# A fused transformer block on one Trainium2 core: six weight loads of the first MLP chunk move from ahead of the out-projection's copies to behind them

## The chip, the core and the metric

The kernel runs on one NeuronCore of one Trainium2 chip. The core has a matrix engine (PE), a vector engine (DVE), an activation engine (ACT), a general engine (POOL) and a sync engine (SP), which in this kernel issues nearly all DMAs, in program order. A DMA that SP has issued runs on the core's 16 DMA engines, and an instruction that needs its data waits on a semaphore. The metric is device time in microseconds (us), lower is better, and a difference is told from no change from about 0.2% on.

## The reference, cut to what matters

```python
x = A_x                                        # 2048 tokens x 640
sa, ca, ga, sb, cb, gb = split(silu(c) @ w_mod)
h = layernorm(x) * (1 + ca) + sa
q, k, v = split(h @ wqkv)                      # 32 heads of 20
o = softmax(q @ k.T / sqrt(20)) @ v            # per head, 2048 x 2048 scores
x = x + ga * (o @ wo)                          # out-projection
h = layernorm(x) * (1 + cb) + sb
out = x + gb * (((h @ w_gate) * (h @ w_up)) @ w_down)   # MLP, 640 -> 1536 -> 640
```

## The kernel before

**Chunks, items, groups.** The 2048 query rows are cut into five chunks of 512, 512, 512, 256 and 256 rows. A chunk has eight items, one for each set of four heads. An item's scores come in units of 128 keys by up to 512 queries; PE writes them into PSUM (L1443), and their exponential is taken either on ACT, two units (later sometimes three) at a time into the tile PP (L1479: one such instruction is an "exp group"), or on DVE, by an integer approximation that goes through the tiles DB and DSS (L1503, L1535, L1540, L1543). PE then multiplies PP or DSS with the values Vf (L2000).

**What follows a chunk.** When an item is done, DVE turns its result out of PSUM (L1627), POOL scales it (L1633), DVE turns it again into OcT (L1641), and four or five DMAs copy OcT's rows to their places in Ocp (L1654). Once a chunk's eight items are in Ocp, `suffix(ci)` follows: eight rounds of the out-projection (PE, L906 with wo and Ocp; the result is added to xck at L1725), a layer norm (L1739 to L1746), five rounds of transposes into h2T (L1758), then for each of 12 column blocks fc a gate round and an up round (L906 with h2T and stg), and the down-projection. All this PE work is laid between the score groups of the next chunk, so the out-projection and MLP of chunk 0 run while chunk 1's exps run.

**The weight blocks.** Gate and up weights come in blocks of 128 columns (160 KB each, L1798) into `stg`, which has three places for gate and three for up blocks. So the first six blocks (fc 0, 1, 2, gate and up) can be requested at once, and each later block must wait until a round has released its place.

**What sets the order.** The program is laid out by a planner at build time. `Sched` simulates the engines with assumed costs, and whenever an engine is free in the simulation it takes the ready task with the lowest priority number whose gate is open. What comes out is a fixed instruction order for each engine, with semaphore waits for every dependence; the simulated times themselves are not in the program. A gate is a number of exp groups: a task may be taken once that many groups have begun in the simulation. Chunk 0 has 512 units, less 4 for each of its 24 quads on DVE, so 416 on ACT, in 208 groups: `gstart[1]`, and with it `gb` of chunk 0, is 208. The gates of chunk 0 that matter here:

| tasks | line | gate | priority on SP |
|---|---|---|---|
| x rows for the residual (xck) | L1704 | gb - 20 = 188 | 15 |
| first six gate and up blocks | L1798 | gb - 10 = 198 | 16.00 to 16.02 |
| copies OcT to Ocp | L1654 | none (ready when OcT is) | 2 |
| first out-projection round | L1732 | gb + 9 = 217 | not on SP |
| first gate round | L1853 | 229, from the same formula at L1697 | not on SP |

On SP lie also, at this place, the projected queries of the last quarter of the tokens: they go from the tile KPB to a DRAM scratch q_rows (L1212, priority 1.5) and come back from it as QT (L1234, priority 1.6) once the rows have landed.

Of the kernel before, what the change touches and what calls it, by code (L numbers as in the profile page):

```python
# [8 lines left out]
BF16 = mybir.dt.bfloat16  # L9
# [7 lines left out]
PV_W = 216.0  # L17
# [100 lines left out]
class Sched:  # L118

    def __init__(self):  # L120
        self.tasks = []
        self.order = {k: [] for k in ("sp", "act", "pe", "dve", "pool")}
        self.all = []
        self.free_at = {k: T0 for k in self.order}
        self.pend = {k: [] for k in self.order}
        self.readyl = {k: [] for k in self.order}
        self.t = 0.0
        self.n = 0
        self.progress = 0
        self.dma_free = 0.0  # L130
        self.pe_mode = None
        self.pe_end = 0.0
        self.pick_pe = None
        self.every = []
        self.ham_w = 0
        self.ham_act = 0.0
        self.cold = True
        self.ncold = 0
        self.nfill = 0
        self.ndup = 0  # L140
        self.nsteal = 0
        self.nx = 0
        self.ng = 1 << 30
        self.hist = []
        self.acts = []
        self.left = 0
        self.lk_end = {"dve": 0.0, "pool": 0.0}
        self.lk_last = None
# [337 lines left out]
GATE_F = (0.468, 0.693, 0.969, 0.732, 1.0)  # L486
FILL_MIN = 4153.722
FILL_HARD = 0.0
FILL_T0, FILL_TH, FILL_MINH = 2300.0, 17000.0, 7500.0
FILL_MODE = 'P'  # L490
DUP_MIN = 0.0
# [54 lines left out]
    39: {"FILL_MIN": 3000, "D_LATE": 17, "PVTOL": 258, "X_LATE": -54.236, "PVCAP": 16},  # L546
}
XHALF = 1
X_LATE = -24.052
X_HALF = 0.0  # L550

# [9 lines left out]
def build_kernel(nc, A_x, A_wqkv, A_wo, B_x, B_w_gate, B_w_up, B_w_down, c, w_mod, out):  # L561
# [7 lines left out]
    NC = len(CHUNKS)  # L569
# [6 lines left out]
    sc = Sched()  # L576
# [14 lines left out]
    def alloc(name, shape, dtype):  # L591
        off = cur[0]
        cur[0] += nb(shape, dtype)
        assert cur[0] <= nc.sbuf_top, f"SBUF overflow at {name}: {cur[0]} > {nc.sbuf_top}"
        return at(name, shape, dtype, off)
# [17 lines left out]
    ps = nc.alloc_psum_tensor("ps_all", [128, 8, 512], F32)  # L613
# [7 lines left out]
    ident = alloc("ident", [128, 128], BF16)  # L621
    mhalf = alloc("mhalf", [128, 4], F32)
    warm = alloc("warm", [128, 1], F32)
    qcol = alloc("qcol", [128, 1], F32)
    c5 = alloc("c5", [KD, 128], BF16)
    csb = alloc("csb", [128, KD], BF16)
# [109 lines left out]
    BPV = 7  # L736
# [15 lines left out]
    def dve(dur, f, deps=(), prio=3.0, **k):  # L752
        return sc.add(Task("dve", dur, f, deps, prio=prio, **k))
# [6 lines left out]
    def pool(dur, f, deps=(), prio=3.0, **k):  # L760
        t = Task("pool", dur, f, deps, prio=prio, **k)
        t.lk = 1
        return sc.add(t)
# [63 lines left out]
    def load_rest():  # L827
# [5 lines left out]
        for q, f in enumerate((first2[0], first2[1],  # L833
# [13 lines left out]
    p_id = pool(300, lambda e: e.affine_select(ident[:], ident[:], pattern=[[-1, 128]], compare_op=ALU.not_equal,  # L847
                                               fill=1.0, base=0, channel_multiplier=1), [p_i0], prio=0)
    p_mh = pool(100, lambda e: e.memset(mhalf[:], -0.5), prio=1)
    p_on = dve(600, lambda e: e.memset(Vf[:, :].rearrange("p (h w) -> p h w", w=VW)[:, :, 0:1], 1.0), prio=-1)  # L850
    d_pz = dve(500, lambda e: e.memset(ps[:, BPV, :], 0.0), [], prio=3.5)
    d_wz = [dve(70, lambda e, w=w: e.memset(w[:, :, D:WKQ], 0.0), prio=0) for w in (wk_sb, wq_sb)]
# [233 lines left out]
    v_last = []  # L1086
# [179 lines left out]
    items = [(ci, j) for ci in range(NC) for j in range(NSET)]  # L1266
# [3 lines left out]
    item_info = {}  # L1270
# [51 lines left out]
    gstart = []  # L1322
# [129 lines left out]
    st_pv = {"item": 0, "free": [d_pz]}  # L1452
# [57 lines left out]
    for qi, (it, us) in enumerate(dquads):  # L1510
# [36 lines left out]
        if X_POOL and qi % X_POOL == X_POOL - 1 and qi < len(dquads) - X_LAST and all(  # L1547
                dquads[z][0] == it for z in range(qi, min(len(dquads), qi + X_TAIL + 1))):
            st_["xby"] = None
            for x in range(X_PIECES):  # L1550
# [5 lines left out]
                t = Task("pool", w * POOL_NS + 180.0, fxp, [tm, te], prio=2.0 + .1 * qi + .01 * x, name=f"XP.{qi}")  # L1556
# [13 lines left out]
            t = term(fx, [tm, te], TT_2X, "X", src=0, last=True)  # L1570
# [106 lines left out]
    def suffix(ci):  # L1677
        alt = NALT and ci >= NC - 2
        bd = bset_done[1 if NALT and ci == NC - 2 else 0]
        hprod, h2T, xck, xn2 = set_r if not alt else set_t if ci == NC - 2 else set_c  # L1680
        first = bd.get("tr", [])
        if alt:
            first = list(sfx_done["qd1"]) if ci == NC - 2 else bd["tr"] + bd["h2T"] + bd["hp"] + bd["out"]
# [3 lines left out]
        tail = ci == NC - 1  # L1687
        qf = full if tail and TAILX else quarters
        t0 = q0 // 128
        gb = int(gstart[ci + 1]) if not tail else 0  # L1690
# [11 lines left out]
        def pr(early=False):  # L1702
            return pbase + rc_[0] - (1500 if tail and early else OPFIRST if early else 0)
        d_xc = dma("sp", 128 * ntl * D * 2, lambda e: e.dma_start(xck[:, 0:ntl, :], xv[:, t0:t0 + ntl, :]),  # L1704
                   (first if alt else bd.get("out", []) + v_last), prio=15, gate=max(0, gb - 20))
        t_xn2 = []
        x1_done = []
        op_last = []
        for tl in range(ntl):
            ev = []  # L1710
            for hf in range(2):
# [12 lines left out]
                def after(r, tl=tl, hf=hf, fx=fx, pq=pq):  # L1724
                    f = lambda e: e.tensor_tensor(xck[:, tl, 320 * hf:320 * hf + 320], ps[:, r.b["b"], 0:320],  # L1725
                                                  xck[:, tl, 320 * hf:320 * hf + 320], ALU.add)
                    if tail and OP_EARLY:
# [5 lines left out]
                          name=f"op{ci}.{tl}")  # L1733
                ev.append(r.evac[0])
                op_last.append(r.last)
            t = t0 + tl
# [52 lines left out]
        for fc in range(FT):  # L1789
            use_x = tail and fc < nsx  # L1790
            wbuf, dm = [], []
            for w_, wv in enumerate((wgv, wuv)):
                cell = {}
                if use_x:
                    cell["t"] = stx[fc][:, w_, :, :]

                def f(e, wv=wv, fc=fc, cell=cell):
                    return e.dma_start(cell["t"], wv[:, :, fc * 128:(fc + 1) * 128])  # L1798
                t = dma("sp", 2 * 128 * KD * 128 * 2, f, sfx_done["qdead"] if use_x and fc < nsq else first if use_x else kp_use if ci == 0 else [], prio=16 + ci + .01 * fc,
                        gate=int(gstart[NC] - 40) if tail and not use_x else 0 if tail else max(0, gb - 10))  # L1800
                if not use_x:
                    t.acq = [(sStg[w_], "s", 1)]

                    def on0(task, cell=cell, w_=w_):
                        cell["i"] = task.slots["s"]
                        cell["t"] = stg[cell["i"]][:, w_, :, :]
                    t.on_start = on0
                wbuf.append(cell)
                dm.append(t)
# [29 lines left out]
            for w_ in range(2):  # L1839
# [5 lines left out]
                if w_ == 0:  # L1845
                    def after(r, gs=gs):
# [3 lines left out]
                        if tail:  # L1850
# [3 lines left out]
                              name=f"g{ci}.{fc}")  # L1854
# [13 lines left out]
        for tl in range(ntl):  # L1868
# [4 lines left out]
            for (c_, w) in cuts:  # L1873
# [10 lines left out]
                if tail and TAILX:  # L1884
# [6 lines left out]
                            prio=1))  # L1891
# [7 lines left out]
    for it in range(len(items)):  # L1899
        ci, j = items[it]  # L1900
# [5 lines left out]
    pvstate = {"sidx": 0, "didx": 0}  # L1906
# [12 lines left out]
    def clk():  # L1919
        return 2.0 if sc.cold else 1.0  # L1920

    def mode_start(mode, t):
        if sc.pe_mode is not None and sc.pe_mode != mode:
            return max(t, sc.pe_end + (PE_BACK if sc.pe_mode == 'S' else PE_SWITCH))
        return max(t, sc.pe_end)

    def s_ready():
        g = pvstate["sidx"]
        if g >= NG:
            return None  # L1930
        ts, us = score_q[g]
        r = 0.0
        for d in ts.deps:
            if d.done is None:
                return None
            r = max(r, d.done + SEM)
        for pool, key, refs in ts.acq:
            a = pool.avail()
            if a is None:
                return None  # L1940
            r = max(r, a[0])
        return r
# [265 lines left out]
    def pick_pe(t):  # L2208
# [4 lines left out]
        if g < NG:  # L2213
# [4 lines left out]
            if (g != HEADG or not HEADG or back[0]) and acquire_ready(ts, t):  # L2218
                start = mode_start("S", t)
# [19 lines left out]
        if dst["next"] < len(dlist) and (g >= NG or due[dst["next"]] + D_LATE < apos[g]):  # L2239
# [3 lines left out]
            if d_attach(ts, t, 1e9, rows, 2, False):  # L2243
                start = mode_start("S", t)
# [17 lines left out]
        sr = s_ready()  # L2262
        if HOLD and sr is not None and t < sr <= t + HOLD and ring() >= RINGLOW:
            return half_x(t)
        if sc.recent(t) < FILL_MIN and ring() >= RINGLOW and pick_x(t, True):
            return True
        if sc.recent(t) < FILL_HARD and t > 20000 and do_fill(t):
            return True
# [6 lines left out]
        it = st_pv["item"]  # L2275
# [32 lines left out]
        if cands and not js and len(cands) >= 2 and (not PV0 or it >= PV0N or len(cands) >= PV0 or cands[0][0] == 'd'):  # L2308
            pv_issue(cands, t)
            return True  # L2310
        if t > FILL_T0 and fill_ok(t, fill_deps):
            return do_fill(t)
        return False

    def do_fill(t):
        mode = FILL_MODE if pvstate["sidx"] else "X"
        start = mode_start(mode, t)
        fs = G
        if pvstate["sidx"] == 0:
            fs = next((q for q in (GX, GC) if q.avail() is not None and q.avail()[0] <= t), GC)  # L2320
        task = Task("pe", 216.0, ffill, fill_deps, ctr="pex", mode=mode, name="fill", acq=[(fs, "g", 1)])
        if not sc.acquire(task, t):
            return False
        b_ = task.slots["g"]
        idb = ident[:].unsqueeze(1).to_broadcast([128, 4, 128])
        if mode == "X":
            task.emits = [lambda e: e.matmul(ps[:, b_, :].rearrange("p (a b) -> p a b", a=4), ident[:], idb)]  # L2327
        else:
            task.emits = [lambda e, x=x: e.matmul(  # L2329
                ps[32 * x:32 * x + 32, b_, :].rearrange("p (a b) -> p a b", a=4), ident[:, 32 * x:32 * x + 32], idb,  # L2330
                tile_position=(0, 32 * x), skip_group_check=True) for x in range(4)]
        sc.activity(start, 512.0)
        sc.left += 1
        sc.finish_issue(task, start, 216.0 * clk())
        fs.done(b_, task)
        sc.pe_mode = mode
        sc.pe_end = start + 216.0 * clk()
        sc.free_at["pe"] = sc.pe_end
        sc.nfill += 1
        return True  # L2340

    fill_deps = [p_id]
    ffill = None

    def fill_ok(t, fdeps):
        if any(d.done is None or d.done + SEM > t for d in fdeps):
            return False
        if xcur[0] is not None and not (PASSDEP or HT0_SPLIT):
            return False
        return sc.recent(t) < (FILL_MINH if t < FILL_TH else FILL_MIN)  # L2350
# [54 lines left out]
```

## Time and profile before

| | us |
|---|---|
| median of 3 runs | 816.97 (816.37 to 817.6) |
| span of the profiled execution, first to last instruction | 821.3 |
| ACT busy in the span | 775.3 (94%), of it 756.2 in 775 exps (L1479) |
| PE busy in the span | 793.6 (97%) |
| DVE busy in the span | 720.4 (88%) |
| six weight blocks issued on SP | 219.87 to 223.15 |
| first out-projection matmul of chunk 0 | 232.33 |
| first gate matmul of chunk 0 | 268.3 |

The profile is of one execution, and it doesn't give that execution's own device time; what lies around its span can only add to it, so it took at least 821.3, and that is 4.3 above the median of the runs. Its times count from the span's start. "Idle before" an instruction is the time its engine had nothing to do ahead of it, and the name behind the arrow is what it waited for. PEclk is the clock that the throttle granted to PE, as a share of full speed. SPq rows are the instructions that issue DMAs; their length is the issue alone, not the transfer.

### The profile page before, as it was taken

The page shows a single profiled execution, that of the slowest core. Times are in us where ns is not written, and L with a number is a line of the kernel's source. Part 1 is how long each engine was busy: PE and PEld are TensorE (multiplying, and loading weights), DVE is VectorE, ACT ScalarE, POOL GpSimd, SP SyncE. Part 2 cuts the span into 40 slices and gives each one's busy share as a digit, 9 for nine tenths or more (in the row PEclk, how much of TensorE's full clock was granted, in tenths as well). Part 3 has the DMA queues.
Part 4 walks back from the last instruction along what each step waited for, and adds up shares of the span by engine and source line. Part 5 has one row for each costly group of instructions (what it writes and reads, how often), then busy time and mean ns, then how long its engine had stood idle before and what let it go on. Part 6 is the DMA issues. An engine that isn't in the chain of part 4 may idle for free.

```text
span 821.3 us, 28879 instructions
## 1 busy us (share of the span) xinstructions
PE 793.6 (97%) x12493; PEld 305.9 (37%) x12493; DVE 720.4 (88%) x1275; ACT 775.3 (94%) x818; POOL 79.1 (10%) x105
## 2 busy tenths in 40 slices
PE   9999999999989999999999999999988999999998
PEld 4433333322223223233233232333143444554567
DVE  7989999899989999999999999998798877667753
ACT  6899999999989999999999999999899999999941
POOL 3300000020002000000011000000011000001000
PEclk9999999999999999999999999999699999999999
DMA  9734211114500235000300222000400236105610
GB/s 292 219 85 104 67 45 40 50 33 123 131 18 25 54 99 138 22 11 23 92 7 6 53 54 54 6 21 23 82 8 10 50 87 134 47 30 127 137 42 17
DMA packets 116445, 54.71 MB, mean 67 GB/s; under 512 B 83915, under 2 KB 116319, under 8 KB 116319
## 3 DMA queue, kind: packets, MB, share of 16 engines
q1 hardware_dynamic: 115391, 51.72, 24.9%
q8 instruction: 99, 1.62, 0.8%
q10 hardware_dynamic: 928, 1.15, 0.4%
q14 instruction: 27, 0.22, 0.1%
HBM read 41.85 MB, written 8.41 MB: 61 GB/s over the span
## 4 chain that ended last, share of the span: by engine, by line
PE 43%; ACT 35%; DVE 15%; issue 7%; DMA 0%; SPq 0%; POOL 0%; DVEq 0%; ACTq 0%; POOLq 0%
ACT PP L1479 34%; PE ps_all L1443 13%; PE ps_all L906 13%; PE ps_all L2000 9%; DVE DB L1503 5%; PE ps_all L902 3%; DVE DSS L1540 3%; DVE DSS L1543 2%; DVE DSS L1535 1%; PE ps_all L2327 1%; PE ps_all L1166 1%; PE ps_all L1102 1%; PE ps_all L1063 1%; DVE wd L1429 1%; DVE gsb L1847 1%
## 5 line engine op out<-in xcount | busy, mean ns | idle before, releaser
L1479 ACT ACTIVATE PP<-ps_all 128x1024 bf16<-128x1024 f32 (+1 forms) x775 | 756.2, 1171 | 11.6 <-PE ps_all L1443 10.0
L1443 PE MATMUL ps_all<-QT,KT 32*128 32x512 bf16 (+1 forms) x2560 | 311.4, 343 | 16.6 <-ACT PP L1479 10.9
L1503 DVE TENSOR_SCALAR DB<-ps_all 128x512 int16<-128x512 f32 x400 | 265.0, 682 | 43.7 <-PE ps_all L1443 42.9
L1443 PEld LDWEIGHTS ps_all<-QT,KT 32*128 32x128 bf16 x2560 | 81.3, 91 | 264.9 <-ACT PP L1479 228.4
L2000 PE MATMUL ps_all<-PP,Vf 128*32 128x512 bf16 (+2 forms) x2084 | 166.0, 346 | 0.4 <-DVE OT L1627 0.4
L1540 DVE TENSOR_TENSOR DSS<-DB,DSS 128x2048 bf16<-128x2048 bf16 x100 | 122.6, 1226 | 0.0
L906 PE MATMUL ps_all<-h2T,stg 128*32 128x512 bf16 (+1 forms) x1740 | 116.8, 347 | 0.9 <-DVE DB L1503 0.2
L1633 POOL TENSOR_TENSOR OTn<-OT,invT 128x512 bf16<-128x512 f32 (+1 forms) x39 | 46.6, 1195 | 604.5 <-DVE invT L1631 604.5
L2000 PE MATMUL ps_all<-DSS,Vf 128*32 128x512 bf16 (+3 forms) x952 | 78.5, 354 | 1.0 <-DVE DSS L1540 0.5
L2000 PEld LDWEIGHTS ps_all<-PP,Vf 128*32 128x32 bf16 (+1 forms) x2084 | 46.0, 94 | 89.8 <-issue 82.0
L1535 DVE TENSOR_SCALAR DSS<-DB 128x2048 int16<-128x2048 int16 x100 | 70.6, 706 | 0.8
L1543 DVE TENSOR_SCALAR DSS<-DB 128x2048 int16<-128x2048 int16 x100 | 69.0, 690 | 0.3 <-PE ps_all L2000 0.3
L906 PE MATMUL ps_all<-wd,hprod 128*32 128x320 bf16 (+1 forms) x1316 | 58.5, 284 | 0.1
L906 PEld LDWEIGHTS ps_all<-h2T,stg 128*32 128x32 bf16 x1740 | 39.2, 96 | 35.0 <-issue 18.2
L906 PEld LDWEIGHTS ps_all<-wd,hprod 128*32 128x32 bf16 x1316 | 31.2, 96 | 16.6 <-issue 7.4
L2000 PEld LDWEIGHTS ps_all<-DSS,Vf 128*32 128x32 bf16 (+1 forms) x952 | 24.0, 95 | 25.1 <-issue 14.3
L906 PE MATMUL ps_all<-wV,hT 128*32 128x320 bf16 (+1 forms) x704 | 32.3, 289 | 0.1
L1166 PE MATMUL ps_all<-hT,wq 128*32 128x512 bf16 x375 | 31.6, 382 | 0.1
L906 PE MATMUL ps_all<-wo,Ocp 128*32 128x320 bf16 (+1 forms) x628 | 28.6, 290 | 1.9 <-DMA Ocp<-OcT 1.8
L2329 PE MATMUL ps_all<-ident 128*32 128x512 bf16 x300 | 28.6, 406 | 0.3 <-DVE DB L1503 0.2
L1847 DVE CAST gsb<-ps_all 128x512 bf16<-128x512 f32 x36 | 24.5, 681 | 3.0 <-PE ps_all L906 3.0
L1627 DVE STREAM_TRANSPOSE OT<-ps_all 128x512 f32<-128x512 f32 (+1 forms) x40 | 24.1, 603 | 2.8 <-PE ps_all L2000 2.7
(122 smaller groups left out, 509.1 us busy)
## 6 DMA issues: line engine op xcount, KB each, us to landing
stg<-in_B_w_gate_dram SPq DMA_DIRECT2D x50, 160.0 KB
stg<-in_B_w_up_dram SPq DMA_DIRECT2D x50, 160.0 KB
QT<-q_rows SPq DMA_DIRECT2D x22, 128.0 KB
KT<-k_rows SPq DMA_DIRECT2D x84, 32.0 KB
wm<-in_w_mod_dram SPq DMA_DIRECT2D x3, 800.0 KB
x<-in_A_x_dram SPq DMA_DIRECT2D x7, 320.0 KB
xck<-in_A_x_dram SPq DMA_DIRECT2D x3, 640.0 KB
wd<-in_B_w_down_dram SPq DMA_DIRECT2D x1, 1920.0 KB
```

What stands on the lines that cost most here:

```text
L906: return lambda e, b: e.matmul(ps[32 * x:32 * x + 32, b, c0 + o:c0 + o + w], lhs()[:, 32 * x:32 * x + 32], rhs() if w == n else rhs()[:, o ...
L1166: f = [lambda e, b_, k=k, x=x: e.matmul(ps[x:x + min(32, w - x), b_, :], wx[:, k, r0 + x:r0 + min(x + 32, w)], hT[tc][:, k, :], tile_posit ...
L1443: ems.append(lambda e, i=i, kt=kt: e.matmul(dstf()[:, i * u.n:(i + 1) * u.n], KT[32 * u.s:32 * u.s + 32, u.j, kt * 128:(kt + 1) * 128], QT ...
L1479: return e.activation(PPs[g % 2][:, cellp["p"], 0:nu * 512], ps[:, b0:b0 + nu, :].rearrange("p b c -> p (b c)"), AFT.Exp, scale=ESCALE)
L1503: return e.tensor_scalar(DB0[:, st_["slot"], x * 512:(x + 1) * 512], bank(cell["b"]), EBIAS, 0.0, op0=ALU.add, op1=ALU.max)
L1535: return e.tensor_scalar(DSS[:, st_["ss"][0], :], DB0[:, st_["slot"], :], 0x7F, 0x3F00, op0=ALU.bitwise_and, op1=ALU.bitwise_or)
L1540: return e.tensor_tensor(d, DB0[:, st_["slot"], :].bitcast(BF16), d, ALU.mult)
L1543: return e.tensor_scalar(DSS[:, st_["ss"][1], :], DB0[:, st_["slot"], :], 0x7F80, 2, op0=ALU.bitwise_and, op1=ALU.bitwise_or)
L1633: f3 = lambda e: e.tensor_tensor(OTn[:, 0:n].rearrange("p (b c r) -> p b r c", c=32, r=2), OT[:, 0:n].rearrange("p (b r c) -> p b r c", c= ...
L1847: f = lambda e: e.tensor_copy(gsb[:, gs, 0:n], ps[:, r.b["b"], 0:n])
L2000: ems.append(lambda e, i=i, kt=kt, stt=stt, stp=stp: e.matmul(ps[32 * s:32 * s + mc, BPV, 0:u.n], Vf[:, (kt * H + 4 * u.j + s) * VW:(kt * ...
L2329: task.emits = [lambda e, x=x: e.matmul(ps[32 * x:32 * x + 32, b_, :].rearrange("p (a b) -> p a b", a=4), ident[:, 32 * x:32 * x + 32], id ...
```

## The change

The gate of the gate and up loads becomes a parameter for chunk 0 (`STG_G0`) and one for the others (`STG_G`). For chunk 0 it goes from gb - 10 to gb + 12, that is from group 198 to group 220. For the other chunks it stays at gb - 10, and the gate of the xck load, now a parameter too, stays at gb - 20.

```diff
+STG_G0, STG_G, XC_G = 12, -10, -20
...
-                   (first if alt else bd.get("out", []) + v_last), prio=15, gate=max(0, gb - 20))
+                   (first if alt else bd.get("out", []) + v_last), prio=15, gate=max(0, gb + XC_G))
...
-                        gate=int(gstart[NC] - 40) if tail and not use_x else 0 if tail else max(0, gb - 10))
+                        gate=int(gstart[NC] - 40) if tail and not use_x else 0 if tail else max(0, gb + (STG_G0 if ci == 0 else STG_G)))
```

The diff also brings a second kind of filler matmul (`zero_fill`), which is off: its threshold `FILL_Z` is 0, so neither its matmuls nor the memset of its tile are emitted.

```diff
+FILL_Z, Z_LATE = 0.0, 0.0
...
+    zt = alloc("zt", [128, 32], BF16)
...
+    p_zt = pool(100, lambda e: e.memset(zt[:], 0.0), prio=5) if FILL_Z > 0.0 else None
...
-        if t > FILL_T0 and fill_ok(t, fill_deps):
-            return do_fill(t)
-        return False
+        if t > FILL_T0 and fill_ok(t, fill_deps) and do_fill(t):
+            return True
+        return FILL_Z > 0.0 and sc.recent(t) < FILL_Z and zero_fill(t)
```

The tile `zt` (64 bytes in each partition) is allocated all the same, so every tile allocated behind it lies 64 bytes further on.

More of the change, by code (lines that the diff above doesn't have):

```diff
@@ L141, in __init__ @@
         self.nsteal = 0
+        self.nzero = 0
         self.nx = 0
@@ L2310, in pick_pe, with zero_fill @@
             return True
-        if t > FILL_T0 and fill_ok(t, fill_deps):
-            return do_fill(t)
-        return False
+        if t > FILL_T0 and fill_ok(t, fill_deps) and do_fill(t):
+            return True
+        return FILL_Z > 0.0 and sc.recent(t) < FILL_Z and zero_fill(t)
+    def zero_fill(t):
+        it = st_pv["item"]
+        if it >= len(items) or pvstate["sidx"] < 2 or not item_info[it]["started"] or t < FILL_TH or p_zt.done is None:
+            return False
+        start = mode_start("P", t)
+        sr = s_ready()
+        if sr is not None and start + PV_W > sr + Z_LATE:
+            return False
+        idb = ident[:].unsqueeze(1).to_broadcast([128, 4, 128])
+        task = Task("pe", 216.0, [lambda e, x=x: e.matmul(
+            ps[32 * x:32 * x + 32, BPV, :].rearrange("p (a b) -> p a b", a=4), zt[:], idb,
+            tile_position=(0, 32 * x), start=False, stop=False, skip_group_check=True) for x in range(4)],
+            [p_zt, p_id], ctr="pep", mode="P", name="zfill")
+        task.seq = 0
+        sc.activity(start, 512.0)
+        sc.left += 1
+        sc.finish_issue(task, start, PV_W * clk())
+        sc.pe_mode = "P"
+        sc.pe_end = start + PV_W * clk()
+        sc.free_at["pe"] = sc.pe_end
+        sc.nzero += 1
+        return True
     def do_fill(t):
```

## The prediction

> **What bounds the kernel now.** I read the page first: the chain that ended last is ACT's exps for 34% of the span and PE for 43%, and ACT is 94% busy. I then asked for the busy time of each engine in stretches of 10 us. From 240 to 570 ACT has almost no gap (0.11 at 320, 0.28 at 480, 0.22 at 540), so there a microsecond that ACT loses is a microsecond of the end. ACT loses much in three places only: 2.67 in 230 to 240, 0.98 + 2.19 in 570 to 590, and 1.29 in 630 to 640. The change lies at the first. The timeline of the SP queue around it (start, length, line, DMA):
>
> ```profile
> 219.87 0.44 SPq L1798 DMA_DIRECT2D stg<-in_B_w_gate_dram  x1
> ...
> 222.62 0.53 SPq L1798 DMA_DIRECT2D stg<-in_B_w_up_dram  x1
> 223.24 1.26 SPq L1212 DMA_DIRECT2D q_rows<-KPB  x2
> 227.16 0.83 SPq L1234 DMA_DIRECT2D QT<-q_rows  x2
> 228.03 3.05 SPq L1654 DMA_DIRECT2D Ocp<-OcT  x4
> 244.47 1.61 SPq L1212 DMA_DIRECT2D q_rows<-KPB  x3
> 247.85 2.85 SPq L1234 DMA_DIRECT2D QT<-q_rows  x4
> ```
>
> The timeline of all engines:
>
> ```profile
> 220.82 0.68 DVE L1178 TENSOR_SCALAR KPB<-ps_all 128x512 bf16<-128x512 f32 x1
> ...
> 223.59 0.43 DVE L1641 STREAM_TRANSPOSE OcT<-OTn 128x256 f32<-128x256 f32 x1
> ...
> 230.18 0.39 PE L1443 MATMUL ps_all<-QT,KT 32*128 32x512 bf16 x2
> ...
> 232.33 0.73 PE L906 MATMUL ps_all<-wo,Ocp 128*32 128x320 bf16 x16 [1.76 <-DMA Ocp<-OcT]
> ...
> 233.65 1.02 ACT L1479 ACTIVATE PP<-ps_all 128x1024 bf16<-128x1024 f32 x1 [1.69 <-PE ps_all L1443]
> ...
> 235.26 1.02 ACT L1479 ACTIVATE PP<-ps_all 128x1024 bf16<-128x1024 f32 x1 [0.59 <-PE ps_all L1443]
> ...
> 236.68 4.70 ACT L1479 ACTIVATE PP<-ps_all 128x1024 bf16<-128x1024 f32 x5 [0.39 <-PE ps_all L1443]
> ```
>
> PE is through at 230.57 and stands until 232.33, because its next instruction is the first out-projection round and the copies to Ocp have not landed. The scores of the next exp are behind that round, so ACT runs dry for 1.69, and then twice more, 0.59 and 0.39: together 2.67. The last two come from the clock. By stretches (PE, PEld, DVE, ACT, POOL busy, then granted clock, DMA share, GB/s):
>
> ```profile
> 230.00:232.00 2.00, 0.57 (x6) 0.10 (x2) 1.53 (x2) 1.96 (x3) 0.00 (x0) 1.00 0.13 31
> 232.00:234.00 2.00, 1.67 (x27) 0.65 (x31) 0.35 (x1) 0.35 (x1) 0.00 (x0) 0.75 0.03 8
> 234.00:236.00 2.00, 2.00 (x26) 0.49 (x18) 1.83 (x4) 1.41 (x2) 0.00 (x0) 0.50 0.02 4
> 236.00:238.00 2.00, 2.00 (x44) 0.78 (x36) 1.09 (x2) 1.61 (x3) 0.00 (x0) 0.90 0.00 0
> ```
>
> PE gets half its clock right after the gap, for about 3.4 us.
>
> **Why the copies are late.** OcT is done at 224.02, yet its copies are issued from 228.03, since SP works in order. KPB is ready at 221.50, but its stores are issued only at 223.24, because SP issues weight blocks until 223.15. The stores end at 224.50, and SP can go on only at 227.16, when they have landed: 2.66 later. The two other places with these stores show 1.77 (246.08 to 247.85) and 1.74 (266.53 to 268.27). What differs is the traffic: the DMA share is 1.25 and 1.08 in 222 to 226, with the weight blocks, and 0.20 (246 to 248) and 0.11 (264 to 268) at the other two.
>
> **The change, part by part.**
>
> *Where the six loads go.* The new gate, 220, opens when the exp of group 219 begins. The profile counts 217 exps up to 224.0 and 222 up to 228.0, so that is at about 226. The copies to Ocp are ready at 224.02, before it, and have priority 2 against 16, so the planner places the loads behind all four. The next SP task is the store at 244.47; six loads at 0.55 each (3.28 before) fill 3.3 us of a hole of 13, so nothing behind them on SP is displaced. Only SP's order changes, then: out of the run behind QT, to behind the fourth copy. The number of DMAs is the same.
>
> *The chain without them.* SP is free at 219.82, after the QT loads. The stores go at 221.54 (KPB plus 0.04, as at 244.43 to 244.47) and end at 222.80. They land 1.75 later, at 224.55 (by the undisturbed rows; by the disturbed one, 2.66, at 225.46). QT: 224.55 to 225.38. Ocp: 225.42 to 228.48 (3.05 long as now). The first round was released 1.20 after the last copy's issue ended (231.09 to 232.29), so now at **229.68**, or 230.59 by the other end. PE gets there at 230.57. The wait of 1.76 is gone, with 0.9 to spare by the one end and 0.02 short by the other.
>
> *The loads' new place.* They go at 228.5 to 231.9. The same six blocks of chunk 1, issued at 391.44, keep the DMA engines busy until about 398, so they take some 7 us: landed by 235.5. The first gate round needs them at 268.3, now 265.6: 30 us of cover. Against the last Ocp copy they come behind it in the queue; if they slowed its landing as they now slow the stores, by 0.9, it would be 230.6, again no wait worth naming. Later blocks wait for a place that a round frees, which doesn't change. By the Trainium skill, "DMA: Bandwidth & Descriptors", section "Rules for kernel authors", a DMA is to be issued early and waited for late. That speaks against this change; here it would price the lost head start, and the rows price it at nothing, since 30 us remain.
>
> *What is late next.* The copies no longer bind; ACT's own exps do. Around chunk 1's first out-projection (419.5, no wait for Ocp) ACT is busy 10.00 of 10 in every stretch, with the same rounds between the same kind of groups. So I take the whole 2.67 as won, and none lost to the next limit.
>
> *The rest.* The filler is off, and no instruction comes of it. Tiles lie 64 bytes further on. No row shows a price for an address; I take 0, from the argument that no shape changes, with 0.1 either way as bound.
>
> **Sum.** ACT saves 1.69 + 0.59 + 0.39 = 2.67. The profiled execution would have a span of 818.6 in place of 821.3; put against the median of the runs, 816.97 - 2.67 = **814.3**. The step from one to the other is not free: the runs are at least 4.3 faster than the profiled execution, so some of its stalls aren't in them. Taking out the two stalls at 570 to 590 and 630 to 640 (3.17 + 1.29 = 4.46) would explain that, and so nearly would the one here with the last (2.67 + 1.29 = 3.96). I take the first, because the stall here follows from the order on a queue and the two others follow no long wait of PE.
>
> **The rivals.**
>
> *Only the wait is won (815.3).* The half clock could be no consequence of the wait, or be absent in the runs. At 574 to 588 and 629 to 632 the clock is halved with no such wait before, so it does come on its own. Then ACT wins 1.69: 816.97 - 1.69 = 815.28. For it also stands a rule: the Trainium skill, "TensorE: Matmul & The Clock Gate", section "Why this matters for your kernels", holds gaps under about 3 us to be harmless to the clock. The trace differs: a gap of 1.76 is followed at once by 0.50. Chance 0.14.
>
> *The stall isn't in the runs, or the copies stay late (817.0).* Without the profiler SP and DMA may be 1.8 us quicker over the 12.5 us from the first load to the landing; then there is nothing to win. For it: the 4.3 above. Against: it needs 14% of a chain made of issues and landings. To this case belongs that the change doesn't do what it says: if OcT came after gate 220 in the planner's time, the loads would stand ahead of the copies, at 226 to 229.5, and their 7 us of traffic would put the landing near 234, for some 818.5. OcT's lead of about 2 us in the trace is against it. Together 0.20.
>
> *The clock moves against it (820.1 to 820.6).* All that follows 230 comes 2.7 earlier, and where the clock drops may move with it. A long drop like that of 574 to 588 costs ACT 3.17. Candidates are 592 to 598 (PE busy 1.54 to 1.65 of 2.00, at full clock) and 610 to 620 (8.28 of 10). With one new drop the time is 814.3 + 3.17 = 817.5, still no change; it is slower from two on, 820.6, or with one where no stall is won, 820.1. For it: three drops in this trace. Against: three runs within 1.2 us of each other. One drop 0.07, slower 0.09.
>
> **Chances and range.** The forecast, 814.3, has 0.50. A measurement of this kernel tells about 0.2% from no change, 1.63 us: faster is below 815.34, slower above 818.60. The second case lies on that edge, so I give 0.08 of its 0.14 to faster. Faster 0.50 + 0.08 = 0.58; same 0.06 + 0.20 + 0.07 = 0.33; slower 0.09. The range goes from 812.8 (the forecast with half of a long drop, 1.5, won as well) to 817.6 (one new drop, with the bound for the addresses); it leaves out the slower cases and a little below.
>
> **What would show it.** Right: on SP the stores to q_rows start about 1.7 sooner after the QT loads and land in under 2; the Ocp copies stand before the six loads; no wait for Ocp ahead of the first L906 with wo; ACT's idle time in 230 to 240 falls from 2.67 to under 0.3; the clock is 1.00 there. Wrong: the stores still take 2.6 to land (then the traffic wasn't the cause); the wait for Ocp is still there; or it is gone and ACT loses as much at another place, which the stretches would show by a clock of 0.50.

## The result, and the profile after

The changed kernel took **814.24 us** (median of 8 runs, 813.85 to 816.65); the kernel before took 817.48 beside it (8 runs, 815.34 to 821.68). The ratio is 0.9952, with a 95% interval of 0.993 to 0.9973. A second comparison gave 814.28 against 816.02 (12 and 34 runs), ratio 0.9986 [0.9967, 1.0005], which doesn't tell the two apart. So the changed kernel's time was the same twice, and what differed was the kernel before: in the profiles the old order stalls in some executions and not in others, and the experiments are about that.

The profiled execution of the changed kernel took 813.85, with a span of 812.1 and full clock throughout. All lines of the source stand up to five further on (L1479 is L1484, L906 is L911). The SP queue around the change, with start, length, line and DMA:

```profile
215.34 4.17 SPq L1239 DMA_DIRECT2D QT<-q_rows  x4
220.90 1.26 SPq L1217 DMA_DIRECT2D q_rows<-KPB  x2
224.00 0.81 SPq L1239 DMA_DIRECT2D QT<-q_rows  x2
224.86 3.05 SPq L1659 DMA_DIRECT2D Ocp<-OcT  x4
227.95 0.48 SPq L1803 DMA_DIRECT2D stg<-in_B_w_gate_dram  x1
...
240.76 1.62 SPq L1217 DMA_DIRECT2D q_rows<-KPB  x3
```

The six loads now stand behind the four Ocp copies. KPB is done at 220.88 and its stores go at 220.90; they end at 222.16 and have landed by 224.00, after 1.84. Before, they went 1.74 behind KPB and took 2.66. The out-projection and ACT in the timelines of the two engines:

```profile
230.09 0.73 PE L911 MATMUL ps_all<-wo,Ocp 128*32 128x320 bf16 x16
```

```profile
215.50 26.84 ACT L1484 ACTIVATE PP<-ps_all 128x1024 bf16<-128x1024 f32 x29
```

The first round has no wait behind it in brackets, and 29 exps follow each other without a gap. The stretches (PE, PEld, DVE, ACT, POOL busy, then granted clock, DMA share, GB/s) show the clock at 1.00 where it was 0.75, 0.50 and 0.90 (232 to 238), and show in the DMA column where the six loads went:

```profile
230.00:232.00 2.00, 1.91 (x35) 0.81 (x35) 1.72 (x3) 2.00 (x3) 0.00 (x0) 1.00 1.21 247
232.00:234.00 2.00, 2.00 (x44) 0.90 (x46) 1.97 (x5) 2.00 (x4) 0.00 (x0) 1.00 0.99 171
234.00:236.00 2.00, 2.00 (x49) 0.83 (x45) 2.00 (x5) 2.00 (x4) 0.00 (x0) 1.00 0.03 7
236.00:238.00 2.00, 2.00 (x36) 0.64 (x28) 2.00 (x4) 2.00 (x3) 1.13 (x2) 1.00 0.04 12
```

**Where the difference of the two profiles lies.** The spans differ by 9.2 (821.3 and 812.1). I lined up single instructions that occur once (the casts to KPB, the transposes to OcT) and took the difference of their start times. It is a staircase: 0.62 from 33 us to 223, 3.6 from 240 to 567, 7.7 from 587 to 612, 9.2 from 638 on, with no drift on the steps. So 0.6 comes in the first 33 us, **3.0 at the stall**, 4.1 at the clock drop of 570 to 590 and 1.5 in 612 to 638. Only the second step is at the place of the change. The same staircase is given for the runs below ("step at the stall", against the changed kernel).

### The profile page after: what moved, and what is told of

It is laid out like the page before. It is cut to its first block, busy times and chain, and to the rows that moved or that the text cites. A ratio compares the mean times of both kernels' runs of the same rounds, so it can differ in the third digit from the quotient of the medians.

```text
span 812.1 us, 28878 instructions
## 1 busy us (share of the span) xinstructions
PE 784.0 (97%) x12493; PEld 305.3 (38%) x12493; DVE 719.8 (89%) x1275; ACT 773.8 (95%) x818; POOL 79.1 (10%) x105
## 4 chain that ended last, share of the span: by engine, by line
PE 40%; ACT 37%; DVE 15%; issue 7%; DMA 1%; ACTq 0%; DVEq 0%
ACT PP L1484 37%; PE ps_all L911 12%; PE ps_all L1448 12%; PE ps_all L2005 9%; DVE DB L1508 5%; PE ps_all L907 3%; DVE DSS L1545 2%; DVE DSS L1548 2%; DVE DSS L1540 1%; PE ps_all L1171 1%; PE ps_all L1107 1%; DMA wm<-in_w_mod_dram 1%; PE ps_all L1068 1%; DVE wd L1434 1%; DVE gsb L1852 1%
## 5 line engine op out<-in xcount | busy, mean ns | idle before, releaser
L1484 ACT ACTIVATE PP<-ps_all 128x1024 bf16<-128x1024 f32 (+1 forms) x775 | 754.7, 1179 | 4.4 <-PE ps_all L1448 3.0
L1448 PE MATMUL ps_all<-QT,KT 32*128 32x512 bf16 (+1 forms) x2560 | 308.1, 340 | 18.1 <-ACT PP L1484 12.4
L2005 PE MATMUL ps_all<-PP,Vf 128*32 128x512 bf16 (+2 forms) x2084 | 164.2, 343 | 0.4 <-DVE OT L1632 0.4
L911 PE MATMUL ps_all<-h2T,stg 128*32 128x512 bf16 (+1 forms) x1740 | 115.9, 345 | 0.9 <-DVE DB L1508 0.2
L911 PE MATMUL ps_all<-wd,hprod 128*32 128x320 bf16 (+1 forms) x1316 | 58.5, 284 | 0.1
L911 PEld LDWEIGHTS ps_all<-h2T,stg 128*32 128x32 bf16 x1740 | 38.9, 95 | 34.6 <-issue 17.6
L911 PEld LDWEIGHTS ps_all<-wd,hprod 128*32 128x32 bf16 x1316 | 31.2, 96 | 16.6 <-issue 7.4
L911 PE MATMUL ps_all<-wV,hT 128*32 128x320 bf16 (+1 forms) x704 | 32.3, 289 | 0.1
L911 PE MATMUL ps_all<-wo,Ocp 128*32 128x320 bf16 (+1 forms) x628 | 28.2, 286 | 0.3
```

What stands on the lines that cost most here:

```text
L911: return lambda e, b: e.matmul(ps[32 * x:32 * x + 32, b, c0 + o:c0 + o + w], lhs()[:, 32 * x:32 * x + 32], rhs() if w == n else rhs()[:, o ...
L1448: ems.append(lambda e, i=i, kt=kt: e.matmul(dstf()[:, i * u.n:(i + 1) * u.n], KT[32 * u.s:32 * u.s + 32, u.j, kt * 128:(kt + 1) * 128], QT ...
L1484: return e.activation(PPs[g % 2][:, cellp["p"], 0:nu * 512], ps[:, b0:b0 + nu, :].rearrange("p b c -> p (b c)"), AFT.Exp, scale=ESCALE)
L2005: ems.append(lambda e, i=i, kt=kt, stt=stt, stp=stp: e.matmul(ps[32 * s:32 * s + mc, BPV, 0:u.n], Vf[:, (kt * H + 4 * u.j + s) * VW:(kt * ...
```

## The experiments

Theory: SP is late behind the QT run, so the six loads push the stores of KPB; the copies to Ocp are late by that and by the traffic; PE waits, and the wait halves its clock. Rival A: the wait and the clock are two things. Rival B: the order on SP hardly matters in most executions, and the measured gain is something else. All ratios are against the kernel before on the same chip.

**The gate alone put back** (in the changed kernel):

```diff
-STG_G0, STG_G, XC_G = 12, -10, -20
+STG_G0, STG_G, XC_G = -10, -10, -20
```

> The changed kernel with the gate of the first six loads put back to gb - 10; what stays of the change is the 64 bytes by which the tiles lie further on. Theory (the six loads hold up the copies to Ocp on SP and in the DMA queue): the wait of PE for Ocp ahead of the first out-projection round is there again, 1.5 to 2.0 us, ACT idles 1.7 to 2.7 us around it, and the time is that of before, 816.5 to 818.5. Rival (the addresses are the cause): no wait, 814.2.

Measured: 816.41 (12 runs, 813.86 to 818.96), ratio 0.9999 [0.9977, 1.0021]. The wait is back, and ACT's breaks with it (1.58 as shown, then 0.59 and 0.47); PE's line and ACT's first in the timeline:

```profile
232.02 0.73 PE L911 MATMUL ps_all<-wo,Ocp 128*32 128x320 bf16 x16 [1.74 <-DMA Ocp<-OcT]
```

```profile
233.25 1.02 ACT L1484 ACTIVATE PP<-ps_all 128x1024 bf16<-128x1024 f32 x1 [1.58 <-PE ps_all L1448]
```

The stores went 1.84 behind KPB and took 2.57 to land; the step at the stall is 2.98. So with the gate back the stall is back. But this profile is of the slowest of the twelve executions, 818.96, and the fastest execution of this kernel, 813.86, is as fast as the changed kernel's, 813.85. The stall is not in all of them.

**PE kept busy in the wait**: 32 matmuls of ident, whose results are not used, ahead of the first out-projection round of the kernel before.

```diff
+        fl = Task("pe", 216.0, [lambda e, x=x: e.matmul(ps[32*x:32*x+32, b_, :]..., ident[:, 32*x:32*x+32], idb,
+            tile_position=(0, 32*x), skip_group_check=True) for _ in range(8) for x in range(4)], ...)
+        sc.all.insert(sc.all.index(op), fl)
```

> The kernel before, with 32 matmuls of the identity (8 sets of four side by side, some 0.22 us a set) laid on PE ahead of the first out-projection round, into the bank which that round then overwrites. PE works through the wait, and the copies come as late as before. Theory (the half clock is a consequence of the wait): the clock stays 1.00 in 230 to 238, the wait for Ocp falls under 0.3 us, ACT idles 1.7 in place of 2.67, and the time is about 816.5, 1 us under before. Rival (the clock drops by itself there): clock 0.50 and ACT idle 2.6 as before, time as before, 817.5.

Measured: 817.51 (815.84 to 820.61), ratio 1.002 [1.0005, 1.0035]. PE, ACT and one stretch:

```profile
230.30 1.91 PE L2364 MATMUL ps_all<-ident 128*32 128x512 bf16 x32
232.63 0.73 PE L907 MATMUL ps_all<-wo,Ocp 128*32 128x320 bf16 x16 [0.42 <-DMA Ocp<-OcT]
```

```profile
233.73 9.27 ACT L1480 ACTIVATE PP<-ps_all 128x1024 bf16<-128x1024 f32 x10 [1.97 <-PE ps_all L1444]
```

```profile
234.00:236.00 2.00, 2.00 (x45) 0.72 (x33) 2.00 (x5) 2.00 (x3) 0.00 (x0) 1.00 0.02 4
```

The copies are still late, but PE stands for 0.42 only, the clock stays at 1.00, and ACT's second and third break are gone. So the half clock followed from the wait, and rival A falls. The time, expected at 816.5, is a miss: the filler itself seems to cost ACT the first break in every execution, wait or no wait, since the fastest, 815.84, stands 1.6 above the fastest of the kernel before (814.26).

**Issues alone, traffic alone.** The six real loads go behind the copies; in their old place stand six loads of 8 KB, or one DMA that moves the same 983 KB from DRAM to DRAM.

```diff
+            t = Task("sp", 400.0, [lambda e, i=i: e.dma_start(zt[:, 32*i:32*i+32], wgv[:, 0, 32*i:32*i+32])], [], nbytes=8192, prio=16.0)
...
+        t = Task("sp", 400.0, [lambda e: e.dma_start(ZD[:, :, 0:128], B_w_gate[:, 0:768].rearrange("r (b n) -> r b n", n=128))], [], nbytes=983040, prio=16.0)
```

> The kernel before with the six loads behind the copies, and in their old place six loads of 8 KB each into a tile that nothing reads: SP's issue time stays there, the traffic of 960 KB goes. Theory (both hold up the copies): the stores to q_rows are issued 3 us after the QT loads as before, but land in 1.8 us in place of 2.66; the wait for Ocp is 0.7 us (0.3 to 0.9), the time 815.0 to 816.0. Rival (SP's issue time alone): wait 1.7, time 817.5. Rival (the traffic alone): no wait, 814.2.

> The kernel before with the six loads behind the copies, and in their old place one DMA that copies as many bytes in pieces of 256 bytes from a weight to a scratch in DRAM: the traffic stays, five of six issues go. Theory (both): the stores are issued as soon as KPB is ready but take 2.4 to 2.9 us to land; the wait for Ocp is 0 to 0.3 us, the time 814.2 to 814.8. Rival (SP's issue time alone): the stores land in 1.8 us, no wait, 814.2. Rival (the traffic alone): wait 1.7, time 817.5.

Measured: 816.26, ratio 0.9999 [0.9979, 1.0018], and 815.71, ratio 0.9998 [0.9984, 1.0013]. Neither profile has a wait, so the forecast wait of 0.3 to 0.9 with the issues did not come, nor the slow landing with the bytes (1.88), and neither tells the two parts apart: SP ended its QT run at 217.30 and 217.25 here, 2.2 to 2.4 sooner than in the changed kernel and in the one with the gate put back (219.51, 219.63). The six issues were over at 220.82, before KPB was done at 221.14, and the bytes had 4 us to move. This was the hint: **SP's lateness differs between executions of the same order.** In the changed kernel one DMA of the QT run took 1.2 longer to issue than its like (4.17 for four against 2.93), and the run started a microsecond later.

The traces show beside what such an issue stands. The page of the profile lists a queue q8, "instruction"; its packets have 16 KB each. In all fourteen profiles one of them starts at 217.8 to 219.4. In the nine in which SP is issuing at that moment, one issue is slow, whichever DMA it is (the last of the QT run in the changed kernel, the fifth weight load with the tile alone), and it ends 0.36 to 0.43 after the packet; in the five in which SP stands idle then, none is. The kernel before and the changed one met another at 206, the tile alone none from 190 up to the loads. Between 30 and 570 us of the fourteen profiles, 126 of 128 issues longer than 1.2 us end 0.29 to 0.48 after the end of such a packet, against 84 of 4860 of those up to 0.9. So SP probably waits there for its own instructions; no run changed that, so it is argued and not shown.

**The change again, and the move by hand without the tile** (six loads moved behind the fourth copy in the kernel before; no 64 bytes are allocated):

```diff
+        for t in six:
+            sc.all.remove(t)
+        p = sc.all.index(oc0[-1]) + 1
+        sc.all[p:p] = six
```

> The changed kernel once more, beside the kernel before on one chip. Theory (lag: the six loads cost only what SP is late by when it reaches them, and that differs between executions): the executions at full clock lie close together, 813.8 to 814.6, while those of before at full clock spread from 814.3 to 816.1; median 814.2 to 815, 1.5 to 2.5 under before. Rival (a fixed cost in each execution): the fastest execution of before is 2.5 or more above the fastest of this.

> The kernel before with the six loads taken out of their place in SP's order and put behind the fourth copy to Ocp, by hand after planning; no new tile, so no 64 bytes. Theory (the place of the loads is all): as the changed kernel, 814.0 to 815.0, no wait for Ocp in the profile. Rival (the addresses matter too): slower than the changed kernel by 0.5 or more.

Measured: 814.28 (813.85 to 818.44), ratio 0.9986 [0.9967, 1.0005], and 815.16 (814.18 to 819.86), ratio 0.9996 [0.9977, 1.0014]. Both profiles have the stores on time (0.02 behind KPB), a landing of 1.85 and 1.88, no wait, and a step of 0.0 at the stall. A cost in every execution is out: the fastest of the kernel before (814.26) is 0.41 above the fastest of the changed kernel, not 2.5. The move by hand misses its forecast (814.0 to 815.0) by a little, and its median is 0.88 above the changed kernel's, as the rival with the addresses had it (0.5 or more); but the fastest executions are 0.33 apart, and how much of the rest is clock drops elsewhere isn't shown. In the mean it can't be told from the kernel before beside it (816.08 and 816.16).

**SP made late**: three loads of 8 KB behind the QT run, once with the six loads in the old place (the diff), once with the six behind the copies as above.

```diff
+        for i in range(3):
+            t = Task("sp", 400.0, [lambda e, i=i: e.dma_start(zt[:, 32*i:32*i+32], wgv[:, 0, 32*i:32*i+32])], [], nbytes=8192, prio=16.0)
+            sc.all.insert(sc.all.index(six[0]), t)
```

> The kernel before with three loads of 8 KB more ahead of the six, about 0.58 us of SP's time each, so 1.7 us later at the six. Theory (lag): the wait for Ocp, 0 to 1.8 us in the kernel before, becomes 1.0 to 3.5 us; the profile shows 3 us or more if SP reaches the six as late as in the first profile; the median is 818 to 819, 2 above before. Rival (a fixed cost, or the clock alone): as before, 816.

> The same three small loads in the same place, with the six loads behind the copies. Theory (lag): SP is through with them before KPB is ready or 0.3 us after, so there is no wait for Ocp, or one under 0.3 us, and the time is that of the changed kernel, 814.0 to 815.0. Rival (any issue in that place costs): 1.7 above the changed kernel.

Measured: **819.99** (11 runs, 815.07 to 823.26), ratio 1.004 [1.0016, 1.0063], against **816.23** (814.21 to 818.6), ratio 1.0006 [0.9991, 1.0021]. SP, PE, ACT and one stretch with the old order (ACT's next breaks are 0.59, 0.47 and 0.60):

```profile
222.66 1.26 SPq L1213 DMA_DIRECT2D q_rows<-KPB  x2
```

```profile
231.68 1.26 PE L907 MATMUL ps_all<-wo,Ocp 128*32 128x320 bf16 x16 [1.36 <-DMA Ocp<-OcT]
```

```profile
233.53 1.02 ACT L1480 ACTIVATE PP<-ps_all 128x1024 bf16<-128x1024 f32 x1 [1.81 <-PE ps_all L1444]
```

```profile
230.00:232.00 2.00, 0.64 (x10) 0.24 (x14) 1.28 (x2) 1.71 (x2) 0.00 (x0) 0.81 0.11 29
```

and with the new order:

```profile
231.53 0.73 PE L907 MATMUL ps_all<-wo,Ocp 128*32 128x320 bf16 x16
```

```profile
214.22 28.64 ACT L1480 ACTIVATE PP<-ps_all 128x1024 bf16<-128x1024 f32 x31
```

The same 1.4 us on SP put the median of the old order 4.0 above before, and that of the new one 0.2 above; the intervals of the ratios overlap a little, at 1.0016 and 1.0021. Compared directly, the means (818.99 and 816.32) lie 2.7 apart, with an interval by resampling of 0.8 to 4.6. In the profiles the stores went 1.41 behind KPB against 0.02, and the step at the stall is 3.9 against 0.0. The new order's 816.23 misses its forecast (814.0 to 815.0): it is 1.95 above the changed kernel, near the 1.7 of the rival that any issue in that place costs. But its profile shows no stall; that execution loses 1.0 to an x load that lands late in the first 33 us, and 0.9 from 745 to 788, and the mean is only 0.2 above that of the move by hand. This pair carries the theory: the price of the old place is set by how late SP is.

**The two parts, with SP late**: the three 8 KB loads, and behind them six more, or the one DMA of 983 KB; the real six behind the copies.

> Here SP is made late by three 8 KB loads behind the QT run, as in the two kernels before, and the issue time of the six weight loads is tested without their bytes: six more 8 KB loads stand in the old place, the six real ones behind the Ocp copies. Theory that the issues alone hold the stores: nine issues of 0.47 to 0.58 end near 222 if the QT run ends near 217, so the stores go 0.8 to 1.5 behind KPB, land in 1.8 to 1.9, and a wait for Ocp of 0.2 to 0.9 is left; time between the pair (816.2 and 820.0), near 817. Rival, that only the traffic matters: the stores may be as late, but no wait ahead of the out-projection, and the time is that of the kernel with the three loads alone, 816.2.

> SP is made late by the same three 8 KB loads; behind them one DMA moves the bytes of the six weight loads (983 KB from DRAM to DRAM in pieces of 256 bytes), and the real six stand behind the copies. One issue more, of about 0.6. Theory that traffic and issues add: the stores are on time (under 0.3 behind KPB) but take 2.5 to 2.7 to land, QT 0.8 later than without, and there is no wait or one under 0.4; time 816 to 817. Rival, that the traffic alone makes the wait: 1 us or more of wait and some 818 or above. If the landing stays at 1.9, the traffic of this DMA is not like that of the six loads, and the run tells nothing of it.

Measured: 815.85 (814.29 to 819.15), ratio 0.9985 [0.9965, 1.0006], and 819.48 (816.95 to 824.83), ratio 1.0025 [1.0001, 1.0049]. SP and PE with the issues alone:

```profile
219.74 4.23 SPq L2373 DMA_DIRECT2D zt<-in_B_w_gate_dram  x9
224.01 1.25 SPq L1213 DMA_DIRECT2D q_rows<-KPB  x2
227.09 0.81 SPq L1235 DMA_DIRECT2D QT<-q_rows  x2
```

```profile
232.26 1.26 PE L907 MATMUL ps_all<-wo,Ocp 128*32 128x320 bf16 x16 [2.22 <-DMA Ocp<-OcT]
```

and with the bytes alone:

```profile
221.50 2.65 SPq L1214 DMA_DIRECT2D q_rows<-KPB  x2
226.58 0.82 SPq L1236 DMA_DIRECT2D QT<-q_rows  x2
```

```profile
231.76 0.73 PE L908 MATMUL ps_all<-wo,Ocp 128*32 128x320 bf16 x16 [1.21 <-DMA Ocp<-OcT]
```

Each part makes a wait alone, in its own way. With the issues, the stores are 3.05 late (KPB is done at 220.96) and land in an undisturbed 1.83. With the bytes they are on time (KPB at 221.46, 0.04 before), but their issue takes 2.65 where it takes 1.26 (the first of the two alone 2.12 instead of 0.74), and the landing 2.43. As to times, the first expectation's wait (0.2 to 0.9) was too small for the profiled execution, whose QT run ended at 219.70 rather than 217. But that execution, 819.15, is the slowest of the twelve, and the median, 815.85, is below even the rival's 816.2: this wait is probably not in most of them, and the times don't tell the two theories apart. The second came out as its rival had it (a wait of 1 or more, 818 or above), but for a reason that neither foresaw: 1.4 of the delay is the stores' issue. So the DMA of 983 KB does more than the six loads, and its 819.48 is no measure of theirs.

**The loads between the stores and the QT loads** (moved to behind the second store, nothing else):

```diff
+        p = sc.all.index(kpb[-1]) + 1
+        sc.all[p:p] = six
```

> The six loads stand between the two stores of KPB and the QT loads that read them back, with no other change. They are then issued while the stores land. Theory: the stores go on time (KPB plus 0.04) whatever SP's lateness, the six issues fill 3.3, so QT can go 0 to 1.6 later than the 2.6 that the stores need in traffic; QT near 226, the copies to 230, the round released near 231.2: a wait of 0.4 to 0.9 in every execution, and often a half clock. Time 815.5 to 817.5. Rival, that SP's order hardly matters as long as the stores are first: no wait, 814.2 to 815.

Measured: 816.69 (815.11 to 820.64), ratio 0.9998 [0.9977, 1.002].

```profile
231.32 0.73 PE L906 MATMUL ps_all<-wo,Ocp 128*32 128x320 bf16 x16 [0.88 <-DMA Ocp<-OcT]
```

The stores are on time, the loads fill SP until 225.93, QT goes at 226.03 and the round waits 0.88, ACT 0.59: as the theory has it. By the theory this wait comes in every execution, since it doesn't depend on SP's lateness; the fastest, 815.11, 0.85 above the fastest of the kernel before, fits that. The clock stays at 1.00.

**The tile alone** (64 bytes, old order):

```diff
+    zt = alloc("zt", [128, 32], BF16)
```

> Only the 64-byte tile is allocated, at the place where the change has it; the order is the old one. In the profiles with that tile the second mcol instruction comes 1.27 to 1.33 after the first, in those without it 1.41 to 1.44, and the fastest executions stand at 813.85 to 813.96 against 814.17 to 814.33. Theory that the tile's place does it: 1.27 to 1.33 here too, fastest executions at 813.9, median as before less 0.3. Rival, that this is chance of few executions: 1.41 to 1.44 and 814.2.

Measured: 816.5 (813.83 to 818.58), ratio 0.9992 [0.9972, 1.0012]. Its profile is the one that speaks most against my forecast's working, because it shows the **old order without the stall**. SP, PE, ACT:

```profile
213.44 2.94 SPq L1235 DMA_DIRECT2D QT<-q_rows  x4
216.42 0.43 SPq L1799 DMA_DIRECT2D stg<-in_B_w_gate_dram  x1
...
220.24 0.72 SPq L1799 DMA_DIRECT2D stg<-in_B_w_up_dram  x1
221.06 1.27 SPq L1213 DMA_DIRECT2D q_rows<-KPB  x2
224.96 0.83 SPq L1235 DMA_DIRECT2D QT<-q_rows  x2
```

```profile
230.12 0.73 PE L907 MATMUL ps_all<-wo,Ocp 128*32 128x320 bf16 x16
```

```profile
214.61 27.75 ACT L1480 ACTIVATE PP<-ps_all 128x1024 bf16<-128x1024 f32 x30
```

The QT run ends at 216.38, over 3 us sooner than in the profile of before (219.82). The six loads are through at 220.96, the stores go 0.16 behind KPB (220.90). They still take 2.63 to land, and the 0.8 of traffic fits into PE's slack. As for the tile, the second mcol instruction comes 1.28 behind the first, as in the three other profiles with this tile (1.27 to 1.33; 1.39 to 1.44 in the ten that have none or a larger one), and the fastest execution is 813.83. The four runs with the tile have fastest executions of 813.83 to 813.86. The kernel before, in 112 executions, has 814.26.

## Why the prediction was right, and where its working was not

**The time, 814.3, was right:** 814.24 and 814.28.

*What bounds the kernel, and the chain on SP.* Right step by step. With all times 0.6 sooner, the stores were to go 0.04 behind KPB (0.02), to land in 1.75 (1.84), QT to go at 223.9 (224.00), the copies to end at 227.9 (227.91). PE finds its operands at 230.09 and waits for nothing.

*The loads' new place.* Right. By the trace no gate or up round waits for its weights (0.2 once before), and nothing behind them on SP is displaced: the next store goes at 240.76, with KPB done at 240.73. The rule of the Trainium skill to issue a DMA early ("DMA: Bandwidth & Descriptors", section "Rules for kernel authors") cost nothing to break here, as the rows had it: 3.3 us of SP ahead of a store, a load and a copy that PE soon waits for were worth more than 8 us of head start with 30 to spare.

*The sum, 2.67: a little too small.* The stall is 3.0 by the staircase. ACT's idle time counts from the end of one exp to the start of the next; but exps that follow each other start 0.91 apart and are 1.02 to 1.32 long here, so they overlap, and a break costs the lost overlap as well. From start to start, the three breaks are 3.01, 1.61 and 1.42, so 3.31 more than three times 0.91. The changed kernel has one of 1.17 at this place, 0.26 more, which leaves 3.05.

*The half clock.* Right: it followed from the wait, as the filler shows. The rule of the Trainium skill that I set as rival ("TensorE: Matmul & The Clock Gate", section "Why this matters for your kernels": no PE gaps above about 3 us between bursts of matmuls, which I read as shorter ones being harmless) doesn't hold here in that reading. By the profiles, a PE gap ahead of this round of 0.42, 0.88 and 1.21 left the clock at 1.00, one of 1.36, 1.74, 1.76 and 2.22 went with 0.50, and no other profile has a half clock here. But the length of the gap alone doesn't decide. In the profiles with 1.36 and 2.22 the clock fell while PE still stood, 0.9 and 1.1 us into the gap (at 231.2 and 231.1), so after less idle time than the 1.21 that left it at 1.00. What does decide wasn't tried.

*Off the median of the runs.* This is the step that failed: "I take the first, because the stall here follows from the order on a queue and the two others follow no long wait of PE." I took the stall for a fixed cost of the order. It is one only when SP comes late out of its QT run. Four profiles have the old order with no load added on SP: before, the gate put back, the filler and the tile alone. Three of them have SP late (QT run ended at 219.82, 219.63, 218.37) and the copies late; the fourth has SP at 216.38 and no wait. (An execution's time is 1.8 above its span in the other profiles, so the profiled one of before took about 823.1, an estimate, which is longer than any of the 112 recorded. The gate put back was profiled in the slowest of its twelve.) Four have the new order and at most the three small loads in the old place: the changed kernel twice, the move by hand, SP made late. None waits, whatever SP did. So the rival "the stall isn't in the runs", at 0.20, is partly true, of a part of the executions.

*What the change is worth, then.* That is known only roughly. Of 104 executions of before whose clock was recorded, 42 had full clock throughout, so no gap of the kind that halves it; of 20 of the changed kernel, 12. If the drops elsewhere come as often in both, the stall with its half clock was in about 1 - 0.404/0.6 = 0.33 of the executions. With the two new orders made by hand counted in (6 of 12, and 4 of 12 with SP late) it is 22 of 44, and 1 - 0.404/0.5 = 0.19. At 3.0 that is 0.6 to 1.0 us in the mean, an estimate. The pooled means are 816.76 and 815.11 (112 and 20 executions), 1.65 apart, ratio 0.998 with an interval by resampling of 0.9971 to 0.999. But the median of before alone was 816.05, 816.02 and 817.08 in the three later comparisons, so pooling mixes in a difference between comparisons; beside each other in the second one, the means are 816.16 and 815.33, 0.83 apart. How the gain divides between the stall and the tile isn't shown by the times. The first comparison's 3.2 was a lucky pair of samples, and a forecast of 814.3 off a median of 816.97 hit in part because the changed kernel's full-clock executions, 813.85 to 814.55, lie there anyway.

*The tile: mis-sized.* I gave the addresses 0.1 either way; the fastest executions say 0.4 in favour. The traces show 0.06 to 0.17 of it, between the two mcol instructions; where the rest lies stays open. In the medians (0.9999 and 0.9992, the two kernels with the tile and the old order) it can't be seen.

*The clock moves against it.* It doesn't move. Drops at 570 to 590 and at 620 to 640 occur with both orders, and in some profiles not at all; by the staircases they are mostly the largest steps beside the stall. The changed kernel, second profile, against the first, in 622 to 624:

```profile
622.00:624.00 2.00, 2.00 (x30) 0.91 (x30) 1.76 (x5) 2.00 (x2) 0.62 (x1) 0.50 0.00 0
```

```profile
622.00:624.00 2.00, 2.00 (x41) 0.96 (x40) 1.84 (x6) 2.00 (x3) 0.62 (x1) 1.00 0.00 0
```

Same program, same PE gap of 0.61 ahead of it, one at 0.50 and the other at 1.00. One such short drop costs 1.4 to 1.5, a long one (10.2 to 13.7 us) 2.7 to 4.3. What decides it was not tried.

## What to carry to other kernels

A queue that works in order passes its lateness on: bulk loads that nobody needs for 30 us, put ahead of a short chain of store, load and copy, cost nothing while the queue is early and several microseconds when it is late. So look at how much slack the queue has in front of them, in more than one execution, and put them behind the chain when there is room. Before a stall in one profile is taken off a median of many runs, find out whether the runs have it: a staircase of start times over a few profiles, and the fastest execution of each kernel, help to tell.

## What the runs showed of the hardware that was not expected

- A DMA's issue on SP is mostly 0.3 to 0.8 us, but single ones take 1.2 to 1.7: the four of the QT run took 2.94 here and 4.17 there. They don't belong to certain DMAs: nearly all end 0.3 to 0.5 after a packet of 16 KB on the instruction queue.
- A PE gap of 1.36 us went with 6.83 us of half clock (231.2 to 238.1, with SP late in the old order), one of 1.21 with none.
- A DMA of 983 KB in flight doubled the issue time of two stores behind it on the same queue, from 1.26 to 2.65; the first of them bore it (2.12 instead of 0.74).
- 64 bytes of address shift ahead of most tiles moved the fastest execution by 0.4 us.
